# An attention and gated-MLP kernel: one 128-partition load of k over q for each pair of heads, the high part of k cast once and copied twice

## The chip, the core and the metric

The kernel runs on one core of a Trainium2 chip. The time of a kernel is the device time of one execution in microseconds (us), and lower is better. The profile shows one more execution, with its own time. It names the engines PE (TensorE matmul; PEld is its weight load), DVE (VectorE), ACT (ScalarE), POOL (GpSimd) and SP (SyncE, which here issues nearly all DMAs; its queue is shown as SPq).

## The reference

Attention with a causal mask and a bias from cumulative sums, over 8 batches of 8 heads (sequence 576, head size 64), and then a gated MLP on its output (model width 512, inner width 1024):

```python
def _attn_ref(q, k, v, s):
    scores = np.matmul(q, k.transpose(0, 1, 3, 2)) / np.sqrt(D)
    cum = np.cumsum(np.maximum(s, 0.0), axis=-1)
    bias = -(cum[:, :, :, None] - cum[:, :, None, :])
    scores = np.where(causal, -1e9, scores + np.minimum(bias, 0.0))
    scores = scores - np.max(scores, axis=-1, keepdims=True)
    attn = np.exp(scores)
    attn = attn / (np.sum(attn, axis=-1, keepdims=True) + 1e-09)
    return np.matmul(attn, v)

def _moe_ref(x, w_in, w_spatial, b_spatial, w_out):
    h = np.maximum(x @ w_in, 0.0)
    u, v = h[..., :512], h[..., 512:]
    v_n = (v - mean(v)) / np.sqrt(var(v) + 1e-06)
    v_s = np.einsum('ts,bsd->btd', w_spatial, v_n) + b_spatial[None, :, None]
    return (u * v_s) @ w_out
```

All inputs are float32 but the four MLP weights, which come as float64 and are turned into two f16 parts on the core.

## The kernel before

The 64 heads are worked in 32 **pairs** of heads, four pairs to a batch, each followed by that batch's share of the MLP. Numbers behind names are pairs (or batches): pb9 belongs to pair 4 (two heads, 8 and 9), KA1 is the second of three buffers.

**From k and q to scores.** The first three pairs (`native_tiles`) multiply k and q as float32. From pair 3 on, k and q are split into a high and a low f16 part, and the scores of a block are two matmuls over 128 rows, KA with QA and then KB with QB (L316). Rows 64 to 127 of KA and of KB both hold the high part of k; rows 0 to 63 of KB hold the low part of k; rows 61 to 63 of KA hold the cumulative sums (`aux_rows`, L214, three small DMAs). Rows 64 to 127 of QA and rows 0 to 63 of QB hold the high part of q, rows 64 to 127 of QB its low part. KA, KB, QA and QB have three buffers each, used in turn, so a buffer is free when the scores of three pairs before are done.

**Loads and splits.** `load_raw` (L226) brings k of a pair twice, to rows 64 to 127 and to rows 0 to 63 of `kraw`, and q to rows 64 to 127 of `qraw` (and to rows 0 to 63 too below pair 6, by N_CD = 6); each of these loads has 64 partitions and 288 KB. `kraw` and `qraw` have one buffer each (N_RB = 1). `split_raw` casts all 128 rows of `kraw` to KB on DVE (L251), subtracts on DVE for the low part (L255), fills KA's rows from `kraw` on ACT (L249, below pair 6) or from KB by a DMA (L257), casts q to QA on ACT (L259), fills QB's rows 0 to 63 on ACT (L261, below pair 6) or by a DMA from QA (L263), and makes the low part of q in four pieces on POOL (L239).

**Softmax and attention.** DVE adds the mask and takes the maximum (L320), ACT takes the exponential with its sum (L326), ACT and DVE write the weights as two f16 parts, pb (L335, L336), and a DMA transpose on SP's queue turns pb to pT (L341). PE multiplies pT with the two parts of v, V1 and V2 (L413; avt, L423, for the last 64 rows), and ACT and DVE write the result as xt (L429, L430). The float32 v is loaded in `fetch_v` (L272, L273) and split in `load_v` (L280).

**MLP of a batch.** vps (L457), its layer norm with hv, mv and rs (L477 to L484), split to vn on ACT and DVE (L490, L491), ups (L507), sps (L520 to L523), the gate g (L525 to L528), ops (L539) and the output. The float64 weights are loaded as words (`fetch_w64`, L158, tile wst) and turned to two f16 parts by four DVE operations (L167 to L174, tile wt), ACT operations and one POOL operation (L153); w_in is worked in eight parts, w_out in four, and all parts of w_out share one wst buffer.

**What sets the order.** Each step gets a position from a table of constants (L23), the list `plan` is sorted by it, and the program is written in that order. The scheduler of the tile framework then orders the instructions of each engine by a simulated timeline, so that the order on an engine follows both the list and the scheduler's own durations. For positions below G_END a dependency without a wait keeps the instructions of an engine behind the last one of the steps marked `first`. Each engine works its instructions strictly in the order so found, and SP issues its DMAs so too. A DMA on SP's queue also waits until the one that is eight places ahead of it has landed, since the DMAs take eight semaphores in turn.

Of the kernel before, what the change touches and what calls it, by code (L numbers as in the profile page):

```python
# [7 lines left out]
F16 = mybir.dt.float16  # L8
# [22 lines left out]
def attn_gated_mlp(ctx, tc, qT, kT, v, s, w_in, w_spT, b_sp, w_out, outT):  # L31
    nc = tc.nc
    P = 128
    NHB, D, H, S = qT.shape
    B, H = NHB // 2, 2 * H
# [77 lines left out]
    def native_tiles(pair):  # L113


        hs = slice(2 * (pair % 2), 2 * (pair % 2) + 2)
        tags = (("g1", "g2"), ("xt1", "xt2"), ("xt1", "xt2"), ("rawk", "rawq"))[pair]
        raw_tiles(pair // 2, hs, tags, (1, 2, 2, N_RB)[pair])
        first_ins["c"] = [raw_rows(pair // 2, hs, nm, 1) for nm in "kq"][1].ins
# [98 lines left out]
    def raw_tiles(hb, hs, tags=("rawk", "rawq"), bufs=1):  # L218

        for tag, nm in zip(tags, "kq"):  # L220
            raws[hb, hs.start, nm] = wk.tile([P, hs.stop - hs.start, S], F32, tag=tag, bufs=bufs, name=f"{nm}raw{hb}")

    def raw_rows(hb, hs, nm, top):
        rows = slice(64 * top, 64 * top + 64)
        if nm == "k" or top or 2 * hb + hs.start // 2 < N_CD:
            return nc.sync.dma_start(out=raws[hb, hs.start, nm][rows], in_=(kT if nm == "k" else qT)[hb, :, hs])  # L226

    def load_raw(hb, pr):
        hs = slice(2 * pr, 2 * pr + 2)
        raw_tiles(hb, hs, bufs=N_RB)  # L230
        for top in (1, 0):
            for nm in "kq":
                raw_rows(hb, hs, nm, top)

    def pieces(eng, out, in0, in1):
        for j in range(2):
            for hf in range(2):
                c = slice(hf * TH, hf * TH + TH)
                eng.tensor_tensor(out=out[:, j, c], in0=in0[:, j, c], in1=in1[:, j, c], op=ALU.subtract)  # L239

    def split_raw(hb, nm, pr):

        p = 2 * hb + pr
        i = p % 3
        raw = raws[hb, 2 * pr, nm]
        lo, hi = slice(0, 64), slice(64, 128)
        if nm == "k":
            if p < N_CD:
                nc.scalar.copy(KA[i][hi], raw[hi])  # L249
            if p < N_KA:  # L250
                nc.vector.tensor_copy(KB[i], raw)  # L251
            else:
                nc.scalar.copy(KB[i], raw)
            eng = nc.gpsimd if p < N_KP else nc.vector
            eng.tensor_tensor(out=KB[i][lo], in0=raw[lo], in1=KB[i][lo], op=ALU.subtract)  # L255
            if p >= N_CD:
                nc.sync.dma_start(out=KA[i][hi], in_=KB[i][hi])  # L257
        else:
            (nc.scalar.copy if p < N_QA else nc.vector.tensor_copy)(QA[i][hi], raw[hi])  # L259
            if p < N_CD:  # L260
                (nc.scalar.copy if p < N_QA else nc.vector.tensor_copy)(QB[i][lo], raw[lo])  # L261
            else:
                nc.sync.dma_start(out=QB[i][lo], in_=QA[i][hi])  # L263
            pieces(nc.gpsimd, QB[i][hi], raw[hi], QA[i][hi])
# [169 lines left out]
    def mlp(b):  # L434
# [32 lines left out]
        for t in range(NC5):  # L467
# [14 lines left out]
            nc.gpsimd.tensor_scalar(rs, mv[:, 1:2], 1.0e-6, None, op0=ALU.add)  # L482
# [7 lines left out]
            nc.scalar.activation(d1, hv, AF.Copy, bias=0.0, scale=SVN)  # L490
            nc.vector.scalar_tensor_tensor(out=d2, in0=hv, scalar=SVN, in1=d1, op0=ALU.mult, op1=ALU.subtract)  # L491
# [84 lines left out]
    for p in range(4):  # L576
# [5 lines left out]
        else:  # L582
            at(l, True, behind, "c", load_raw, 1, p % 2)
            for nm in "kq":
                at((0, 0, O_S2, O_S3)[p], True, split_raw, 1, nm, p % 2)
# [100 lines left out]
```

## Time and profile before

| | before |
|---|---|
| median of 3 runs | 735.04 us (731.93, 736.01, 735.04) |
| profiled execution | 736.15 us, its span 734.4 us |
| mean granted clock of TensorE | 0.944 |
| kraw loads, qraw loads | 61 and 35, 288.0 KB each |
| KA from KB, QB from QA by DMA | 26 and 26, 144.0 KB each |
| DMA in all | 119.10 MB, mean 162 GB/s |

The span goes from the first to the last instruction; 1.75 us of the profiled time lie outside of it. "Busy" is the time in which an engine has an instruction at work; an engine that is not busy waits for the one that the trace names behind an arrow. Loads of k, q and v are counted in KB of 1024 bytes, rates in units of 10^9 bytes each second.

### The profile page before, as it was taken

The numbers are of one execution on the slowest core, as the hardware profiler recorded it, in microseconds if no ns is written. First come the engines' busy times: TensorE is split into PE (matmuls) and PEld (weight loads), VectorE is DVE, ScalarE is ACT, GpSimd is POOL, SyncE is SP. The second block draws the span as 40 slices with busy tenths as digits, with TensorE's granted clock in tenths as the row PEclk, the third lists the DMA queues.
The fourth block names the chain that finished last, engine by engine and source line by source line (L and its number), as shares of the span: only waits on it lengthen the run. The fifth ranks groups of instructions, "written<-read, shape, count | busy, mean of one in ns | idle before, by whom it ended". The sixth has DMA issues, their size and how long they took to land. (4 is left out here: it accounts for less than half of the span.)

```text
span 734.4 us, 15985 instructions
## 1 busy us (share of the span) xinstructions
PE 633.7 (86%) x5696; PEld 408.8 (56%) x5696; DVE 606.4 (83%) x1660; ACT 525.1 (72%) x1334; POOL 186.5 (25%) x226
## 2 busy tenths in 40 slices
PE   4563737867656999999999999999999999999998
PEld 2232314634324577656765676476656765677576
DVE  8977998889998769898998999889988997872431
ACT  5975768667579568878787878788778888762322
POOL 7000464443022312233223322242224220100100
PEclk9986778988878999999999999999999999999999
DMA  8899957678989939898999699978996888450001
GB/s 200 193 203 213 216 148 160 110 169 184 212 189 188 203 70 188 185 206 137 213 185 227 133 188 168 237 160 170 189 231 163 159 170 184 84 109 34 33 12 65
DMA packets 243262, 119.10 MB, mean 162 GB/s; under 512 B 213887, under 2 KB 227373, under 8 KB 243182
## 3 DMA queue, kind: packets, MB, share of 16 engines
q1 hardware_dynamic: 243182, 118.08, 77.0%
q8 instruction: 45, 0.74, 0.4%
q14 instruction: 35, 0.29, 0.1%
HBM read 46.71 MB, written 9.44 MB: 76 GB/s over the span
## 5 line engine op out<-in xcount | busy, mean ns | idle before, releaser
L239 POOL TENSOR_TENSOR QB<-qraw,QA 64x288 f16<-64x288 f32 x116 | 127.5, 1129 | 321.3 <-ACT QA L259 273.4
L326 ACT ACTIVATE p<-psS,mx 128x512 f32<-128x512 f32 (+3 forms) x256 | 132.7, 524 | 50.7 <-DVE mx L320 27.0
L320 DVE CUSTOM_DVE_ANT_0 psS<-psS,mb 128x128 f32<-128x128 f32 (+3 forms) x320 | 154.2, 492 | 16.5 <-PE psS L316 13.8
L336 DVE SCALAR_TENSOR_TENSOR pb<-p,sm,pb 128x384 f16<-128x384 f32 (+3 forms) x256 | 136.3, 566 | 10.5 <-ACT pb L335 9.6
L335 ACT ACTIVATE pb<-p,sm 128x384 f16<-128x384 f32 (+3 forms) x256 | 122.7, 554 | 21.2 <-DVE sm L331 9.9
L539 PE MATMUL ops<-g,wo 128*128 128x288 f16 x768 | 108.1, 290 | 10.2 <-DVE g L525 4.4
L413 PE MATMUL av<-pT,V 128*64 128x128 f16 (+2 forms) x960 | 84.5, 294 | 34.1 <-DMA pT<-pb 28.6
L457 PE MATMUL vps<-win,xt 128*128 128x512 f16 (+1 forms) x576 | 102.7, 352 | 12.7 <-ACT p L326 7.7
L520 PE MATMUL sps<-ws,vn 128*128 128x288 f16 x768 | 108.4, 289 | 0.7 <-DVE vn L491 0.7
L507 PE MATMUL ups<-xt,win 128*128 128x288 f16 x768 | 102.4, 287 | 0.0
L316 PE MATMUL psS<-KA,QA 128*128 128x128 f16 (+3 forms) x348 | 85.4, 316 | 13.4 <-ACT p L326 11.8
L539 PEld LDWEIGHTS <-wo 128*128 128x128 f16 x768 | 74.5, 99 | 37.5 <-issue 12.0
L316 PE MATMUL psS<-KB,QB 128*128 128x128 f16 (+4 forms) x348 | 89.8, 312 | 0.4 <-DVE KB L255 0.4
L413 PEld LDWEIGHTS <-V 128*64 128x64 f16 x960 | 52.0, 116 | 66.4 <-issue 48.0
L520 PEld LDWEIGHTS <-vn 128*128 128x128 f16 x768 | 74.3, 99 | 26.3 <-issue 2.9
L507 PEld LDWEIGHTS <-win 128*128 128x128 f16 x768 | 73.4, 98 | 23.3 <-issue 2.4
L457 PEld LDWEIGHTS <-xt 128*128 128x128 f16 (+1 forms) x576 | 46.9, 103 | 60.6 <-issue 20.7
L482 POOL TENSOR_SCALAR rs<-mv 128x1 f32<-128x1 f32 x40 | 12.4, 310 | 168.1 <-DVE mv L481 154.3
L316 PEld LDWEIGHTS <-QA 128*128 128x128 f16 (+1 forms) x348 | 29.4, 102 | 39.6 <-issue 32.1
L326 ACT ACTIVATION_READ_ACCUMULATOR p<-psS,mx 128x1 f32 x256 | 51.3, 201 | 0.0
L527 ACT CAST g<-g 128x288 f16<-128x288 f32 x64 | 27.3, 427 | 31.6 <-DVE g L525 31.5
L255 DVE TENSOR_TENSOR KB<-kraw,KB 64x1152 f16<-64x1152 f32 x29 | 45.7, 1576 | 0.2
(117 smaller groups left out, 876.8 us busy)
## 6 DMA issues: line engine op xcount, KB each, us to landing
kraw<-in_kT_dram SPq DMA_DIRECT2D x61, 288.0 KB
qraw<-in_qT_dram SPq DMA_DIRECT2D x35, 288.0 KB
out_dram<-ob SPq DMA_DIRECT2D x32, 288.0 KB
vraw<-in_v_dram SPq DMA_DIRECT2D x16, 512.0 KB
wst<-in_w_in_dram SPq DMA_DIRECT2D x8, 512.0 KB
QB<-QA SPq DMA_DIRECT2D x26, 144.0 KB
KA<-KB SPq DMA_DIRECT2D x26, 144.0 KB
vraw<-in_v_dram SPq DMA_DIRECT2D x16, 128.0 KB
```

The costliest lines, as they stand in the source:

```text
L239: eng.tensor_tensor(out=out[:, j, c], in0=in0[:, j, c], in1=in1[:, j, c], op=ALU.subtract)
L255: eng.tensor_tensor(out=KB[i][lo], in0=raw[lo], in1=KB[i][lo], op=ALU.subtract)
L316: nc.tensor.matmul(ps[m, c0:c0 + w], U[i][:, g, q0:q0 + n], T[i][:, g, k0:k0 + w], start=st, stop=not st)
L320: nc.vector.tensor_tensor_reduce(out=ps[:, c0:c0 + w], in0=ps[:, c0:c0 + w], in1=mask, op0=ALU.add, op1=ALU.min, scale=-0.125, scalar=3.0e ...
L326: nc.scalar.activation(p32, ps[:, c0:c0 + w], AF.Exp, bias=mx[:, col:col + 1], scale=-1.0, accum_out=sm[:, acc:acc + 1])
L335: nc.scalar.activation(dst[:, off:off + w], p32, AF.Copy, bias=0.0, scale=sm[:, col:col + 1])
L336: nc.vector.scalar_tensor_tensor(out=dst[:, n + off:n + off + w], in0=p32, scalar=sm[:, col:col + 1], in1=dst[:, off:off + w], op0=ALU.mul ...
L413: nc.tensor.matmul(dst, V[i][:, jc, h + j], rhs, start=jc == n == 0 and q0 > 0, stop=jc == 3 and n == 2)
L457: nc.tensor.matmul(ps[m, 0:w], xx[:, c, t * P:t * P + (m.stop - m.start)], ww[:, c, NF + g * w:NF + g * w + w], start=c == n == 0, stop=c ...
L507: nc.tensor.matmul(ps[:, 0:TH], ww[:, c, fs], xx[:, c, ts], start=n == 0, stop=n == 3 * KC - 1)
L520: nc.tensor.matmul(ps[:, 0:TH], vv[:, c, fs], ww[:, c, ts], start=n == 0, stop=False)
L539: nc.tensor.matmul(ps[:, 0:TH], ww[:, f, ms], gg[:, f, ts], start=n == 0, stop=n == 3 * FC - 1)
```

## The change

For each pair from pair 3 on, the host lays k over q in one array (`kqT`), and one load of 128 partitions (576 KB, tile `raw`, two buffers) brings k to rows 0 to 63 and q to rows 64 to 127. DVE casts k once, to the tile `kh` (64 rows, one buffer); two DMAs copy kh to rows 64 to 127 of KA and of KB; DVE subtracts kh from raw for the low part. For q, ACT writes QA as before, a DMA fills QB's rows 0 to 63 for every pair, and the four POOL pieces stay. ACT's casts of L249 and L261 are gone. In the layer norm the factor 64 moves to the POOL operation that makes rs, so ACT makes the first part of vn with a copy and DVE the second with a plain subtraction. The table of constants is the same; N_CD, N_KA, N_QA, N_KP and N_RB are not used any more. Nothing else of what is computed changes.

```diff
--- before.py
+++ after.py
@@ -215,53 +215,40 @@
 
     raws = {}
 
-    def raw_tiles(hb, hs, tags=("rawk", "rawq"), bufs=1):
-
-        for tag, nm in zip(tags, "kq"):
-            raws[hb, hs.start, nm] = wk.tile([P, hs.stop - hs.start, S], F32, tag=tag, bufs=bufs, name=f"{nm}raw{hb}")
-
-    def raw_rows(hb, hs, nm, top):
-        rows = slice(64 * top, 64 * top + 64)
-        if nm == "k" or top or 2 * hb + hs.start // 2 < N_CD:
-            return nc.sync.dma_start(out=raws[hb, hs.start, nm][rows], in_=(kT if nm == "k" else qT)[hb, :, hs])
-
-    def load_raw(hb, pr):
-        hs = slice(2 * pr, 2 * pr + 2)
-        raw_tiles(hb, hs, bufs=N_RB)
-        for top in (1, 0):
-            for nm in "kq":
-                raw_rows(hb, hs, nm, top)
-
-    def pieces(eng, out, in0, in1):
-        for j in range(2):
-            for hf in range(2):
-                c = slice(hf * TH, hf * TH + TH)
-                eng.tensor_tensor(out=out[:, j, c], in0=in0[:, j, c], in1=in1[:, j, c], op=ALU.subtract)
-
-    def split_raw(hb, nm, pr):
-
-        p = 2 * hb + pr
+    def raw_tiles(hb, hs, tags):
+
+        for (tag, bufs), nm in zip(tags, "kq"):
+            raws[hb, hs.start, nm] = wk.tile([P, 2, S], F32, tag=tag, bufs=bufs, name=f"{nm}raw{hb}")
+
+    def raw_rows(hb, hs, nm):
+        src = kqT[hb, 0:64, hs] if nm == "k" else kqT[hb, 64:128, hs]
+        return nc.sync.dma_start(out=raws[hb, hs.start, nm][64:128], in_=src)
+
+    def load_raw(p):
+
+        hb, pr = divmod(p, 2)
+        raws[p] = wk.tile([P, 2, S], F32, tag="raw", bufs=2, name=f"raw{p}")
+        nc.sync.dma_start(out=raws[p], in_=kqT[hb, :, 2 * pr:2 * pr + 2])
+
+    def split_raw(nm, p):
+
+
         i = p % 3
-        raw = raws[hb, 2 * pr, nm]
+        raw = raws[p] if nm == "k" else raws.pop(p)
         lo, hi = slice(0, 64), slice(64, 128)
         if nm == "k":
-            if p < N_CD:
-                nc.scalar.copy(KA[i][hi], raw[hi])
-            if p < N_KA:
-                nc.vector.tensor_copy(KB[i], raw)
-            else:
-                nc.scalar.copy(KB[i], raw)
-            eng = nc.gpsimd if p < N_KP else nc.vector
-            eng.tensor_tensor(out=KB[i][lo], in0=raw[lo], in1=KB[i][lo], op=ALU.subtract)
-            if p >= N_CD:
-                nc.sync.dma_start(out=KA[i][hi], in_=KB[i][hi])
+            kh = wk.tile([64, 2, S], F16, tag="kh", bufs=1, name=f"kh{p}")
+            nc.vector.tensor_copy(kh, raw[lo])
+            nc.sync.dma_start(out=KA[i][hi], in_=kh)
+            nc.sync.dma_start(out=KB[i][hi], in_=kh)
+            nc.vector.tensor_tensor(out=KB[i][lo], in0=raw[lo], in1=kh, op=ALU.subtract)
         else:
-            (nc.scalar.copy if p < N_QA else nc.vector.tensor_copy)(QA[i][hi], raw[hi])
-            if p < N_CD:
-                (nc.scalar.copy if p < N_QA else nc.vector.tensor_copy)(QB[i][lo], raw[lo])
-            else:
-                nc.sync.dma_start(out=QB[i][lo], in_=QA[i][hi])
-            pieces(nc.gpsimd, QB[i][hi], raw[hi], QA[i][hi])
+            nc.scalar.copy(QA[i][hi], raw[hi])
+            nc.sync.dma_start(out=QB[i][lo], in_=QA[i][hi])
+            for j in range(2):
+                for c in (slice(0, TH), slice(TH, S)):
+                    nc.gpsimd.tensor_tensor(out=QB[i][hi, j, c], in0=raw[hi, j, c], in1=QA[i][hi, j, c],
+                                            op=ALU.subtract)
 
     vraws = {}
@@ -479,7 +466,8 @@
                 nc.sync.dma_start(out=st[0:64, 1], in_=st[64:128, 0])
                 nc.sync.dma_start(out=st[64:128, 1], in_=st[0:64, 0])
             nc.vector.bn_aggr(out=mv, in_=st if tail else st[:, 0])
-            nc.gpsimd.tensor_scalar(rs, mv[:, 1:2], 1.0e-6, None, op0=ALU.add)
+
+            nc.gpsimd.tensor_scalar(rs, mv[:, 1:2], 1.0e-6, 1.0 / (SVN * SVN), op0=ALU.add, op1=ALU.mult)
             nc.gpsimd.tensor_tensor(out=rs, in0=rs, in1=mhalf, op=ALU.pow)
             nc.vector.tensor_scalar(hv, hv, mv[:, 0:1], rs, op0=ALU.subtract, op1=ALU.mult)
             if tail:
@@ -487,8 +475,8 @@
                 d2 = wk.tile([P, w], F16, tag="tl", bufs=1, name=f"tl{b}")
             else:
                 d1, d2 = vn1[:, t], vn2[:, t]
-            nc.scalar.activation(d1, hv, AF.Copy, bias=0.0, scale=SVN)
-            nc.vector.scalar_tensor_tensor(out=d2, in0=hv, scalar=SVN, in1=d1, op0=ALU.mult, op1=ALU.subtract)
+            nc.scalar.copy(d1, hv)
+            nc.vector.tensor_tensor(out=d2, in0=hv, in1=d1, op=ALU.subtract)
             if tail:
                 for g in range(2):
                     m, gs = slice(64 * g, 64 * g + 64), slice(g * w, g * w + w)
@@ -580,9 +568,9 @@
             at(l, True, native_sel, p)
             at((-19.9, -18.9, O_S2, O_S3)[p], True, native_cum, p)
         else:
-            at(l, True, behind, "c", load_raw, 1, p % 2)
+            at(l, True, behind, "c", load_raw, p)
             for nm in "kq":
-                at((0, 0, O_S2, O_S3)[p], True, split_raw, 1, nm, p % 2)
+                at((0, 0, O_S2, O_S3)[p], True, split_raw, nm, p)
     at(-19.95, True, prefix_sums)
     at(O_I1, True, init_static, 0)
     at(O_I0, True, init_static, 1)
@@ -596,10 +584,10 @@
     for hb in range(2, NHB):
         lag = LAGS if hb < 4 else LAG
         for pr in range(2):
-            at(4 * hb + 2 * pr - O_LR + (LAGR if hb < 4 else LAG), False, load_raw, hb, pr)
+            at(4 * hb + 2 * pr - O_LR + (LAGR if hb < 4 else LAG), False, load_raw, 2 * hb + pr)
             at(4 * hb + 2 * pr - O_LD + lag, False, aux_rows, 2 * hb + pr)
             for n, nm in enumerate("kq"):
-                at(4 * hb + 2 * pr - O_LD + lag + D_LD * n, False, split_raw, hb, nm, pr)
+                at(4 * hb + 2 * pr - O_LD + lag + D_LD * n, False, split_raw, nm, 2 * hb + pr)
         at(4 * hb - O_LV + (LAGV if hb < 4 else LAG), False, fetch_v, hb)
         at(4 * hb - O_LV + (LAGV if hb < 4 else LAG), False, load_v, hb)
     for c in range(KC):
@@ -660,8 +648,7 @@
 
     B, H, S, D = inputs['q'].shape
     lay = {
-        'qT': inputs['q'].reshape(2 * B, H // 2, S, D).transpose(0, 3, 1, 2),
-        'kT': inputs['k'].reshape(2 * B, H // 2, S, D).transpose(0, 3, 1, 2),
+        'kqT': _np.concatenate([inputs[n].reshape(2 * B, H // 2, S, D).transpose(0, 3, 1, 2) for n in 'kq'], axis=1),
         'v': inputs['v'].transpose(0, 2, 1, 3).reshape(B, S, H * D),
         's': inputs['s'].reshape(B * H, S),
         'w_in': inputs['moe_w_in'],
```

As the scheduler orders the changed program anew, rows move on several engines. Three places follow.

SP's queue at the start, before. The rows stand between the loads of pairs 0 to 3 and the second attention transpose; vraw0 and vraw1 are v of the first two half-batches, wst parts of w_in, kraw2 and qraw2 belong to pair 4, pT0 is the first transpose.

```order
L158 DMA wst_328<-in_w_in_dram 128x1024
L272 DMA vraw0_330<-in_v_dram 128x4x256
L273 DMA vraw0_330<-in_v_dram 128x256
L158 DMA wst_333<-in_w_in_dram 128x1024
L341 DMA_TRANSPOSE pT0_176<-pb0_146 128x20x128
L272 DMA vraw1_514<-in_v_dram 128x4x256
L273 DMA vraw1_514<-in_v_dram 128x256
L341 DMA_TRANSPOSE pT('t', 0)_192<-pb4_0_182 128x10x128
L158 DMA wst_521<-in_w_in_dram 128x1024
L226 DMA kraw2_523<-in_kT_dram 64x1152
L226 DMA qraw2_524<-in_qT_dram 64x1152
L341 DMA_TRANSPOSE pT1_221<-pb1_194 128x20x128
```

The same place now, from the second wst load on (raw4 and raw5 are the loads of pairs 4 and 5):

```order
L158 DMA wst_331<-in_w_in_dram 128x1024
L259 DMA vraw1_512<-in_v_dram 128x4x256
L260 DMA vraw1_512<-in_v_dram 128x256
L158 DMA wst_519<-in_w_in_dram 128x1024
L231 DMA raw4_521<-in_kqT_dram 128x1152
L158 DMA wst_545<-in_w_in_dram 128x1024
L231 DMA raw5_599<-in_kqT_dram 128x1152
L158 DMA wst_601<-in_w_in_dram 128x1024
L214 DMA KA1_77<-cc_112 1x2x576 x3
L214 DMA KA2_78<-cc_112 1x2x576
L328 DMA_TRANSPOSE pT0_176<-pb0_146 128x20x128
L328 DMA_TRANSPOSE pT('t', 0)_192<-pb4_0_182 128x10x128
```

The first transpose stood behind two wst loads and v of the first half-batch; now v of the second half-batch, three more wst loads and the loads of pairs 4 and 5 stand ahead of it too, and the next transpose follows it at once.

SP's queue around the copies of pairs 6 and 7 now, where there were loads of k and q and copies from KB before (psS4 names the scores of pair 4, which read KA1):

```order
L242 DMA KA0_76<-kh6_1205 64x1152
L192 DMA wsp_st_822<-in_w_spT_dram 128x576
L243 DMA KB0_103<-kh6_1205 64x1152
L231 DMA raw8_1159<-in_kqT_dram 128x1152
L214 DMA KA1_77<-cc_112 1x2x576 x3
L247 DMA QB1_101<-QA1_74 64x1152
L242 DMA KA1_77<-kh7_1530 64x1152
L243 DMA KB1_104<-kh7_1530 64x1152
```

DVE's rows at the same time, from the cast of pair 7 to that of pair 8:

```order
L241 CAST kh7_1530<-raw7_811 64x1152
L307 ISA psS4_959,mx4_907<-psS4_959,mb4_90 128x128
L307 ISA mx4_907 128x1
L150 SCALAR_TENSOR_TENSOR ws2_121<-wsp_st_822,ws1_120 128x576
L468 BN_AGGR mv0_0_1052<-st0_0_1051 128x2
L468 BN_AGGR mv0_1_1085<-st0_1_1084 128x2
L307 ISA psS4_1001,mx4_907<-psS4_1001,mb_85 128x384
L307 ISA mx4_907 128x1
L244 TENSOR_TENSOR KB1_104<-raw7_811,kh7_1530 64x1152
L365 TENSOR_TENSOR mx4_907<-mx4_907 128x1
L317 TENSOR_SCALAR sm4_908<-sm4_908 128x4 x2
L241 CAST kh8_1708<-raw8_1159 64x1152
```

The cast to kh8 needs the one kh buffer, so it waits until both copies of kh7 have landed, and those stand behind the small KA1 loads on SP, which wait for the scores of pair 4. The wait is new: before, the cast wrote KB itself.

DVE around the last split of w_out, before (wt_1515; pb17 is the second head of pair 8):

```order
L170 SCALAR_TENSOR_TENSOR wt_1515<-wst_1513,wt_1515 128x512
L336 SCALAR_TENSOR_TENSOR pb17_2070<-p32_17_2071,sm8_1876,pb17_2070 128x384
L336 SCALAR_TENSOR_TENSOR pb17_2070<-p32_17_2071,sm8_1876,pb17_2070 128x512
L336 SCALAR_TENSOR_TENSOR pb17_2070<-p32_17_2071,sm8_1876,pb17_2070 128x128
L378 TENSOR_TENSOR mx9_2152<-mx9_2152 128x1
L336 SCALAR_TENSOR_TENSOR pb17_2070<-p32_17_2071,sm8_1876,pb17_2070 128x256
L320 ISA psS9_2344,mx9_2152<-psS9_2344,mb_85 128x384
L320 ISA mx9_2152 128x1
L330 TENSOR_SCALAR sm9_2153<-sm9_2153 128x4
L174 SCALAR_TENSOR_TENSOR wt_1515<-wst_1513,wt_1515 128x512
```

And now (wt_1499; pb16 is the first head of pair 8):

```order
L170 SCALAR_TENSOR_TENSOR wt_1499<-wst_1497,wt_1499 128x512
L318 RECIPROCAL sm8_1861<-sm8_1861 128x1
L323 SCALAR_TENSOR_TENSOR pb16_1862<-p32_16_1863,sm8_1861,pb16_1862 128x512
L307 ISA psS9_2140,mx9_2136<-psS9_2140,mb_85 128x384
L307 ISA mx9_2136 128x1
L323 SCALAR_TENSOR_TENSOR pb16_1862<-p32_16_1863,sm8_1861,pb16_1862 128x128
L323 SCALAR_TENSOR_TENSOR pb16_1862<-p32_16_1863,sm8_1861,pb16_1862 128x256
L317 TENSOR_SCALAR sm8_1861<-sm8_1861 128x4
L174 SCALAR_TENSOR_TENSOR wt_1499<-wst_1497,wt_1499 128x512
```

The last step of the split stood behind the four weights of pb17, and stands now behind those of pb16, ahead of pb17: it was DVE's row 493 and is row 471. On PE, the matmuls ops of batch 0 that read the last parts of w_out (tile ops0_11) had 24 psS, 30 av and 30 avt matmuls more ahead of them before than now: the scores and the attention of one pair. From the third ups tile of batch 1 on (ups1_10), PE has issued the same scores in both programs, and its order is nearly the same from there to the end.

More of the change, by code (lines that the diff above doesn't have):

```diff
@@ L30, in attn_gated_mlp @@
 @with_exitstack
-def attn_gated_mlp(ctx, tc, qT, kT, v, s, w_in, w_spT, b_sp, w_out, outT):
+def attn_gated_mlp(ctx, tc, kqT, v, s, w_in, w_spT, b_sp, w_out, outT):
     nc = tc.nc
     P = 128
-    NHB, D, H, S = qT.shape
-    B, H = NHB // 2, 2 * H
+    NHB, D, H, S = kqT.shape
+    B, H, D = NHB // 2, 2 * H, D // 2
     NPAIR = H // 2
@@ L116, in native_tiles @@
         hs = slice(2 * (pair % 2), 2 * (pair % 2) + 2)
-        tags = (("g1", "g2"), ("xt1", "xt2"), ("xt1", "xt2"), ("rawk", "rawq"))[pair]
-        raw_tiles(pair // 2, hs, tags, (1, 2, 2, N_RB)[pair])
-        first_ins["c"] = [raw_rows(pair // 2, hs, nm, 1) for nm in "kq"][1].ins
+        tags = ((("g1", 1), ("g2", 1)), (("xt1", 2), ("xt2", 2)), (("xt1", 2), ("xt2", 2)))[pair]
+        raw_tiles(pair // 2, hs, tags)
+        first_ins["c"] = [raw_rows(pair // 2, hs, nm) for nm in "kq"][1].ins
     def native_sel(pair):
```

## The prediction

> **What bounds the kernel now.** I read the page's shares first, then the span in 40 slices, and then busy time by stage.
>
> ```profile
> PE 633.7 (86%) x5696; PEld 408.8 (56%) x5696; DVE 606.4 (83%) x1660; ACT 525.1 (72%) x1334; POOL 186.5 (25%) x226
> PE   4563737867656999999999999999999999999998
> DVE  8977998889998769898998999889988997872431
> DMA  8899957678989939898999699978996888450001
> ```
>
> PE leads by busy time, but not everywhere. A slice is 734.4 / 40 = 18.4 us: for the first thirteen slices (239 us) PE has digits of 3 to 8, and from there 9s to the end. DVE and the DMA engines have 7s to 9s where PE has not. Cut into stages (us, then busy us of each engine with its instructions, the granted clock, the DMA share, GB/s):
>
> ```profile
> 0.00:85.00 85.00, 45.26 (x327) 23.08 (x329) 72.77 (x194) 61.55 (x145) 18.26 (x30) 0.85 0.95 201
> 85.00:239.00 154.00, 101.39 (x831) 61.07 (x829) 140.20 (x350) 110.97 (x272) 56.50 (x51) 0.82 0.80 174
> 239.00:650.00 411.00, 406.26 (x3843) 266.02 (x3842) 364.61 (x1054) 326.05 (x856) 107.45 (x136) 1.00 0.86 173
> 650.00:734.40 84.40, 80.79 (x702) 58.67 (x700) 28.82 (x64) 26.54 (x62) 4.25 (x10) 1.00 0.17 47
> ```
>
> The columns after the length are PE, PEld, DVE, ACT, POOL. Up to 85 us the DMA engines are full (0.95); to 239 us DVE is the fullest engine (140.20 of 154, 91%); from 239 to 650 us PE has 4.7 us of idle time in 411, and in the chain that ended last PE stands alone from 604 us on. So **whatever this change gives or takes must arise in the first 239 us**, and PE then carries it to the end one for one. The order of PE after that place is nearly the same in both programs, which leaves no other source. In the later stages the fewer bytes and six ACT casts can save at most those 4.7 us, and I count nothing: PE is the cover, and DVE has 411.00 - 364.61 = 46 us of room before it would show.
>
> **What the early stage waits for.** The waits between 20 and 245 us (total, times, longest), by engine and releaser:
>
> ```profile
> PE av L413 <- DMA pT<-pb: 27.2, 12, 5.6
> ACT pb L335 <- DMA pT<-pb: 6.0, 2, 4.2
> DVE KB L251 <- DMA kraw<-in_kT_dram: 4.5, 3, 1.9
> ```
>
> Transposes and loads both come late. How fast a load is depends on its shape. The first row is the DMA view from 3 to 11 us, when loads of k and q with 64 partitions are nearly all that is issued or under way; the second is from 17 to 20 us, when the loads under way are wst and v, with 128 partitions.
>
> ```profile
> DMA packets 457, 1.71 MB, mean 214 GB/s; under 512 B 85, under 2 KB 85, under 8 KB 457
> DMA packets 744, 1.04 MB, mean 345 GB/s; under 512 B 36, under 2 KB 643, under 8 KB 744
> ```
>
> The engines are full both times, so the same bytes take 1.6 times as long with 64 partitions.
>
> **Term A, the loads of the start: -4.4 us.** Issues up to 85 us, KB each:
>
> ```profile
> qraw<-in_qT_dram SPq DMA_DIRECT2D x9, 288.0 KB
> kraw<-in_kT_dram SPq DMA_DIRECT2D x7, 288.0 KB
> ```
>
> These are k and q of the pairs 0 to 4 and q of pair 5: 16 x 294,912 B = 4.72 MB, at 214 GB/s 22.0 us of full DMA engines. Now there are six such loads (8.3 us), three raw loads of 589,824 B (1.77 MB at 345 GB/s, 5.1 us) and three copies of 147,456 B for pair 3 (at 214 GB/s, for want of a nearer row, 2.1 us): 15.5 us, or **6.6 us less**. That is the most; the least is nothing, where DVE hides it. DVE has no room in most of the start and has some in other parts:
>
> ```profile
> 10.00:15.00 5.00, 5.00 (x19) 2.22 (x18) 3.50 (x8) 3.31 (x6) 1.30 (x3) 1.00 1.03 218
> 25.00:30.00 5.00, 2.94 (x9) 1.22 (x9) 5.00 (x19) 4.53 (x15) 0.00 (x0) 1.00 0.80 139
> 55.00:60.00 5.00, 1.07 (x11) 1.07 (x12) 2.10 (x7) 1.01 (x2) 0.00 (x0) 0.58 0.95 196
> ```
>
> From 25 to 30 us DVE is full, and an earlier load buys nothing there. From 10 to 15 and from 55 to 60 us DVE is idle for 1.5 and 2.9 us while the DMA engines are full. I take these two holes, 4.4 us, as what earlier data can close.
>
> A rule of the Trainium skill (page "DMA: Bandwidth & Descriptors", section "Rules for kernel authors") says that two transfers to disjoint halves of the partitions serialize, because both use the same 16 engines, and advises one 128-partition transfer. Read strictly, only bytes count then, and the start would save (4.72 - 3.98) MB at 201 GB/s = 3.7 us in place of 6.6. The trace speaks for more, since its two rates differ.
>
> **Term B, the splits from 85 to 239 us: -1.3 us.** raw has two buffers, so a load can be issued while the pair before is still being split: DVE's three waits of 4.5 us go. The work on DVE and POOL stays the same, by these rows:
>
> ```profile
> L251 DVE CAST KB<-kraw 128x1152 f16<-128x1152 f32 x29 | 23.4, 809 | 6.0 <-DMA kraw<-in_kT_dram 6.0
> L255 DVE TENSOR_TENSOR KB<-kraw,KB 64x1152 f16<-64x1152 f32 x29 | 45.7, 1576 | 0.2
> L491 DVE SCALAR_TENSOR_TENSOR vn<-hv,vn 128x512 f16<-128x512 f32 x32 | 21.8, 682 | 2.6 <-ACT vn L490 2.5
> L528 DVE TENSOR_TENSOR g<-g,g 128x288 f16<-128x288 f32 x64 | 33.0, 516 | 7.7 <-ACT g L527 7.7
> ```
>
> The cast has half the partitions and as many elements on each, so I leave it at 809 ns. The subtraction has the same form. The plain subtraction for vn is not in the trace with 512 columns; by the ns for each column of L255 (1576 / 1152 = 1.37) it takes 700 ns, by those of L528 (516 / 288 = 1.79) 917, by those of the cast (0.70) 360, against 682 now. Four of them (batch 0) lie before 239 us: from -1.3 to +0.9 us; I take 0, by L255, the nearest in form. ACT's copy for vn and the second constant of POOL's rs change nothing that I can read off any row; ACT is 72% busy in this stage (110.97 of 154.00) and POOL 37%, which hides some tenths on each.
>
> New is the **wait for the one kh buffer**: the cast to kh(p+1) waits until both copies of kh(p) have landed, and DVE with all its masks, weights and norms queues behind it. The tightest place is kh8, eleven rows after kh7 on DVE. SP's issue times and the way of a small DMA are in these rows (SP's two, then DVE's that uses the copy):
>
> ```profile
> 61.64 2.32 SPq L214 DMA_DIRECT2D KA<-cc  x3
> 150.81 0.59 SPq L480 DMA_DIRECT2D st<-st  x1
> 152.61 0.21 DVE L481 BATCH_NORM_AGGREGATE mv<-st 128x2 f32<-128x12 f32 x1
> ```
>
> The KA1 loads can only be issued after the last scores of pair 4, about when DVE masks them. Then: three KA loads 2.3 us, QB 0.6, and KA 0.6 and KB 0.6 for kh7, then 1.8 us from the last issue to use (152.61 - 150.81, an upper end) and 147,456 B / 201 GB/s = 0.7 us more: 6.6 us. Against it DVE has the last mask row of pair 4 with its reading, the subtraction and two or three small rows: five at its mean of 606.4 / 1660 = 0.365 us, and 1.2 us more for the subtraction, 3.0 us. **The stall is 3.6 us at the dearest**, less if SP is early. Later pairs have 20 rows and more between their casts, so I price only this one, at 3.2 (SP's 0.4 us of slack taken off): -4.5 + 3.2 = -1.3. The ends are -4.5 and +3.6.
>
> **Term C, the last split of w_out: -2.5 us.** The last w_out split gates the ops of batch 0, after which PE has no more idle time to speak of:
>
> ```profile
> 229.43 0.54 PE L539 MATMUL ops<-g,wo 128*128 128x288 f16 x3 [0.16 <-POOL wo L153]
> 234.29 2.83 PE L539 MATMUL ops<-g,wo 128*128 128x288 f16 x12
> 606.50 0.54 PE psS L316 x4
> 672.36 1.10 PE av L413 x18
> 625.80 0.47 PE avt L423 x30
> ```
>
> On DVE that split stands 493 - 471 = 22 rows earlier, 22 x 0.365 = 8.0 us. But in return the matmuls of one pair are behind it instead of ahead: by the last three rows 24 x 0.135 + 30 x 0.061 + 0.47 = 5.5 us, work that PE did while it had to wait anyway. -8.0 + 5.5 = **-2.5**; the ends are -8.0 (PE finds other holes for it) and 0.
>
> **The sum.** -4.4 - 1.3 - 2.5 = -8.2 us against the profiled execution's own 736.15 (span 734.4, and 1.75 around it): **728.0 us**. That execution lies 1.1 above the median of the runs, 735.04, within their spread.
>
> **Rivals.**
>
> *Nothing comes through.* DVE, 86% busy to 85 us and 91% to 239 us, hides A, and C cancels, since both move the same work around one engine: only -1.3 is left, 734.9. For it: DVE is full in most 5-us pieces of the start, and its work is unchanged. Against it: its holes are where DMA is full.
>
> *The change doesn't cut DMA work.* The loads of a pair fall from 864 to 576 KB, but the copies inside the core grow from 288 to 432 KB from pair 6 on, and from none to 432 for pairs 3 to 5. If a copy costs as much as a 64-partition load, a pair of the first three goes from 4 x 294,912 B / 214 = 5.5 us to 1.7 + 2.1 = 3.8, and the gain of A shrinks to 5 us or less for three pairs, spread beyond 85 us. This ends between the first rival and the forecast, near 732; the forecast's range holds it.
>
> *Slower: the first transpose is held back.* SP works in order, and pT0 now stands behind 8.06 MB of loads in place of 4.80 MB. The arrivals of transposes on PE, and SP's first issues of them:
>
> ```profile
> 29.98 0.32 PE L413 MATMUL av<-pT,V 128*64 128x384 f16 x1 [1.55 <-DMA pT<-pb]
> 43.67 1.17 PE L413 MATMUL av<-pT,V 128*64 128x384 f16 x16 [1.73 <-DMA pT<-pb]
> 84.84 3.36 PE L413 MATMUL av<-pT,V 128*64 128x384 f16 x29 [1.67 <-DMA pT<-pb]
> 24.92 3.20 SPq L341 DMA_TRANSPOSE pT<-pb  x1
> 29.41 2.45 SPq L341 DMA_TRANSPOSE pT('t', 0)_192<-pb  x1
> ```
>
> The 3.26 MB more take 16.2 us at 201 GB/s, so pT0 (29.98) may land at 46.2, and behind it the tail transpose and pT1, with 2.45 and 3.20 us of issue, at 51.9 in place of 43.67: 8.2 us late. ACT's writing of pb waits for such a landing (the row of 6.0 us above), DVE waits for ACT, and the delay goes through. It decides if **pT1 lands later than 43.67**. Then A is +8.2 in place of -4.4, and B and C stay: 736.15 + 8.2 - 1.3 - 2.5 = **740.6**. Against it: the 3.26 MB are not extra, they stood between later transposes before, and by the last transpose of the start (84.84) both programs have loaded about as much, 10.4 and 10.3 MB by the shapes in SP's order. The loads ahead are also faster now.
>
> *Better than forecast.* A in full (-6.6), no stall at kh8 (B -4.5), C as it is: 722.6, and with C in full (-8.0) 717.0.
>
> **Chances.** A measurement of this kernel can tell about 0.5% from no change, 3.7 us: 731.4 to 738.7. Forecast, with the rival of unchanged DMA work beside its upper end: 0.50 (722.6 to 731.4). Better still: 0.08. Nothing comes through: 0.24. Slower by the first transpose: 0.18 (738.7 to 744). So faster 0.58, same 0.24, slower 0.18. The range goes from 718, near the sum of the best ends, to 741, which takes in the slower rival's own time; beyond both ends about 0.15 to 0.2 is left.
>
> **What would show it.** A right: loads of raw at over 300 GB/s, DVE's holes at 10 to 15 and 55 to 60 us smaller, pT1 on PE before 43.67 and pT7 before 84.84. A wrong: pT1 later than that, with a longer wait of ACT on pT. B right: no wait of the cast on a load from 85 us on, and one wait of some 3 us on a copy of kh at kh8; wrong: many such waits, 1 us and more at each cast. C right: ops0_11 on PE near 220.6 (234.29 less 8.0 and less the 5.7 of A and B), and PE gapless behind it. The whole is wrong if PE shows more than 5 us of idle time after its ops of batch 0, or if the distance from there to the end differs from that of before by more than the 5.5 us that were moved.

## The result, and the profile after

The changed kernel is **slower**: 759.54 us median (751.79 to 763.07, 4 runs) against 735.52 us (731.93 to 738.17, 4 runs) for the kernel before, a ratio of 1.0315 (95% interval 1.0224 to 1.0407). The profiled execution took 763.07 us, its span is 761.3 us, 26.9 us longer than before.

The page of the changed kernel has DVE busy for 8 us less, but PE for 21 us longer with as many matmuls (654.9 us against 633.7, 5696 each), and PE's digits differ where it was gapless before:

```profile
PE 654.9 (86%) x5696; PEld 414.2 (54%) x5696; DVE 598.3 (79%) x1660; ACT 519.8 (68%) x1328; POOL 181.9 (24%) x226
PE   4764457987689998989899898989998999999998
DVE  9879997687986979689787887789879897963331
DMA  9988756577687787957777767968995776451001
```

Busy time by stage of the changed kernel (columns as in the prediction):

```profile
0.00:85.00 85.00, 49.46 (x342) 26.93 (x342) 74.81 (x197) 58.60 (x143) 22.42 (x29) 0.79 0.89 208
85.00:239.00 154.00, 114.77 (x849) 65.32 (x843) 129.69 (x340) 106.68 (x264) 56.96 (x56) 0.80 0.72 165
239.00:650.00 411.00, 382.81 (x3545) 245.81 (x3545) 342.75 (x988) 306.67 (x802) 95.08 (x125) 0.98 0.75 159
```

Up to 239 us PE did more than before (49.5 + 114.8 us against 45.3 + 101.4). From 239 to 650 us its idle time rose from 4.7 to 28.2 us, and DVE's from 46 to 68 us, while the DMA engines have less to do (0.75 against 0.86). So the loss is neither in the start nor a matter of bytes.

The first ups matmuls of a batch are a milestone that both traces show. First of before, batch 1 and batch 7, then of the changed kernel:

```profile
257.48 3.11 PE L507 MATMUL ups<-xt,win 128*128 128x288 f16 x24
693.35 11.93 PE L507 MATMUL ups<-xt,win 128*128 128x288 f16 x96
```

```profile
246.86 1.63 PE L495 MATMUL ups<-xt,win 128*128 128x288 f16 x12
720.45 11.93 PE L495 MATMUL ups<-xt,win 128*128 128x288 f16 x96
```

At batch 1 the changed kernel is **10.6 us ahead**; from there to batch 7 it needs 473.6 us where the kernel before needs 435.9, **37.7 us more**; -10.6 + 37.7 = +27.1, the whole difference. A little of the 10.6 is moved work: 35 matmuls of scores and attention that stood ahead of this milestone before come behind it now, and at the third ups tile, from which on PE's order is nearly the same, the lead is 9.3 us (252.08 against 261.41).

The stretch between the two milestones, before and then now, splits the 37.7 us:

```profile
257.48:693.35 435.87, 431.13 (x4110) 284.73 (x4108) 369.03 (x1064) 330.24 (x865) 103.07 (x132) 1.00 0.79 161
246.86:720.45 473.59, 447.27 (x4143) 288.73 (x4142) 378.46 (x1091) 339.48 (x888) 101.06 (x138) 0.98 0.69 147
```

PE's idle time grew from 4.7 to 26.3 us, and PE was busy 16.1 us longer for nearly as many matmuls, at a granted clock of 0.98 in place of 1.00.

The group of the cast to kh says what DVE stood still for (busy, mean ns, then the idle time just before it with its releasers), and the view of waits says how much of it lies between 239 and 650 us (total, times, longest):

```profile
L241 DVE CAST kh<-raw 64x1152 f16<-64x1152 f32 x29 | 22.8, 785 | 47.9 <-DMA KB<-kh 37.5 <-DMA KA<-kh 5.9 <-issue 3.7
```

```profile
DVE kh L241 <- DMA KB<-kh: 31.0, 12, 5.1
DVE kh L241 <- DMA KA<-kh: 5.9, 2, 3.6
DVE kh L241 <- issue: 3.7, 1, 3.7
PE psS L303 <- ACT q L313: 15.8, 10, 2.5
```

15 of the 19 casts of that stage wait, 40.6 us in all. This is DVE's time and not PE's, so that it lies near the 37.7 us of loss proves nothing yet; the paced kernel below is the test. PE's longest wait there (the last line) is for ACT's exponentials, which wait for DVE's maxima. One pair in the middle, pair 23 and the cast of pair 24, on DVE, POOL and SP, and at the end what waited behind it on ACT and PE (start, us, what, idle time before):

```profile
442.51 0.75 DVE L241 CAST kh<-raw 64x1152 f16<-64x1152 f32 x1 [0.57 <-DMA KB<-kh]
454.81 3.14 SPq L328 DMA_TRANSPOSE pT<-pb  x1
456.57 1.35 DVE L244 TENSOR_TENSOR KB<-raw,kh 64x1152 f16<-64x1152 f32 x1
456.59 4.74 POOL L250 TENSOR_TENSOR QB<-raw,QA 64x288 f16<-64x288 f32 x4 [15.07 <-ACT QA L246]
458.04 1.37 SPq L328 DMA_TRANSPOSE pT('t', 20)_5643<-pb  x1
461.35 0.36 SPq L231 DMA_DIRECT2D raw<-in_kqT_dram  x1
462.40 0.53 SPq L242 DMA_DIRECT2D KA<-kh  x1
463.03 0.54 SPq L243 DMA_DIRECT2D KB<-kh  x1
467.87 0.75 DVE L241 CAST kh<-raw 64x1152 f16<-64x1152 f32 x1 [3.69 <-issue]
468.92 0.47 ACT L313 ACTIVATE p<-psS,mx 128x256 f32<-128x256 f32 x1 [3.60 <-DVE mx L307]
470.76 0.38 PE L303 MATMUL psS<-KA,QA 128*128 128x512 f16 x1 [2.30 <-ACT q L313]
```

The cast of pair 23 runs at 442.5, but KA and KB of that pair are free only when the scores of pair 20 are done, at 456 us (counting DVE's mask rows against the program's order, the last of pair 20 starts at 455.9). On SP the copies stand behind two transposes and behind the raw load of pair 25, which waits for POOL's pieces; they are issued at 462.4 and 463.0, behind 576 KB, and 4.8 us after the last issue the next cast goes, after 3.7 us of standstill. (For this one cast the trace names no releaser; that it waited for the copies is read from the one kh buffer and from the rows of its neighbours.) By the same count the first mask row of pair 24 comes at 526.0: no score needed its cast for another 58 us, and yet all of DVE's rows behind it waited. ACT waited 3.60 us for one of them and PE 2.30 us for ACT, and from 470 to 475 us the granted clock is 0.68, where it was 1.00 from 440 to 470. The chain that ended last passes through the same kind of wait at the cast of pair 29:

```profile
565.52 0.36 SPq L231
565.93 4.88 DMA KA<-kh
570.81 0.55 issue
571.36 0.75 DVE kh L241
```

### The profile page after: what moved, and what is told of

It reads as the page before. It is cut to its first block, busy times and chain, and to the rows that moved or that the text cites. A ratio compares the mean times of both kernels' runs of the same rounds, so it can differ in the third digit from the quotient of the medians.

```text
span 761.3 us, 15918 instructions
## 1 busy us (share of the span) xinstructions
PE 654.9 (86%) x5696; PEld 414.2 (54%) x5696; DVE 598.3 (79%) x1660; ACT 519.8 (68%) x1328; POOL 181.9 (24%) x226
## 2 busy tenths in 40 slices
DMA packets 243038, 114.83 MB, mean 151 GB/s; under 512 B 213471, under 2 KB 226957, under 8 KB 242958
## 5 line engine op out<-in xcount | busy, mean ns | idle before, releaser
L250 POOL TENSOR_TENSOR QB<-raw,QA 64x288 f16<-64x288 f32 x116 | 118.6, 1052 | 261.2 <-ACT QA L246 151.6
L313 ACT ACTIVATE p<-psS,mx 128x128 f32<-128x128 f32 (+3 forms) x256 | 132.7, 523 | 60.2 <-DVE mx L307 35.6
L323 DVE SCALAR_TENSOR_TENSOR pb<-p,sm,pb 128x384 f16<-128x384 f32 (+3 forms) x256 | 133.2, 555 | 7.7 <-ACT pb L322 7.3
L444 PE MATMUL vps<-win,xt 128*128 128x512 f16 (+1 forms) x576 | 107.0, 359 | 14.6 <-POOL win L153 9.7
L400 PE MATMUL av<-pT,V 128*64 128x128 f16 (+2 forms) x960 | 91.0, 300 | 32.4 <-DMA pT<-pb 20.5
L508 PE MATMUL sps<-ws,vn 128*128 128x288 f16 x768 | 113.0, 298 | 3.3 <-DVE g L513 2.6
L495 PE MATMUL ups<-xt,win 128*128 128x288 f16 x768 | 106.2, 291 | 0.0
L303 PE MATMUL psS<-KB,QB 128*128 128x128 f16 (+3 forms) x348 | 91.5, 314 | 0.0
L444 PEld LDWEIGHTS <-xt 128*128 128x128 f16 (+1 forms) x576 | 47.5, 104 | 64.3 <-issue 27.1
L470 POOL TENSOR_SCALAR rs<-mv 128x1 f32<-128x1 f32 x40 | 16.0, 401 | 199.6 <-DVE mv L468 174.5
L241 DVE CAST kh<-raw 64x1152 f16<-64x1152 f32 x29 | 22.8, 785 | 47.9 <-DMA KB<-kh 37.5
L515 ACT CAST g<-g 128x288 f16<-128x288 f32 x64 | 27.1, 428 | 40.5 <-DVE g L513 40.4
L303 PEld LDWEIGHTS <-QA 128*128 128x128 f16 (+1 forms) x348 | 30.0, 103 | 45.3 <-issue 39.1
```

Of the source, the lines that this page charges most:

```text
L250: nc.gpsimd.tensor_tensor(out=QB[i][hi, j, c], in0=raw[hi, j, c], in1=QA[i][hi, j, c], op=ALU.subtract)
L303: nc.tensor.matmul(ps[m, c0:c0 + w], U[i][:, g, q0:q0 + n], T[i][:, g, k0:k0 + w], start=st, stop=not st)
L313: nc.scalar.activation(p32, ps[:, c0:c0 + w], AF.Exp, bias=mx[:, col:col + 1], scale=-1.0, accum_out=sm[:, acc:acc + 1])
L323: nc.vector.scalar_tensor_tensor(out=dst[:, n + off:n + off + w], in0=p32, scalar=sm[:, col:col + 1], in1=dst[:, off:off + w], op0=ALU.mul ...
L400: nc.tensor.matmul(dst, V[i][:, jc, h + j], rhs, start=jc == n == 0 and q0 > 0, stop=jc == 3 and n == 2)
L444: nc.tensor.matmul(ps[m, 0:w], xx[:, c, t * P:t * P + (m.stop - m.start)], ww[:, c, NF + g * w:NF + g * w + w], start=c == n == 0, stop=c ...
```

## The experiments

Each was timed beside the kernel before; ratios are against that. The kernel before took 738.1 to 739.5 us at the median in these sessions and 735.5 beside the changed kernel, so 3 or 4 us between runs of different sessions say little. "The changed kernel" is the base unless another is named. Every edit also makes the scheduler order the rows of all engines anew, so a run shows an edit together with its new order.

**Two kh buffers** (`e1_kh2_g1`) and its control (`e2_g1`). The first theory, K, was that the number of kh buffers decides.

```diff
-            kh = wk.tile([64, 2, S], F16, tag="kh", bufs=1, name=f"kh{p}")
+            kh = wk.tile([64, 2, S], F16, tag="kh", bufs=2, name=f"kh{p}")
...
-            g32 = wk.tile([P, TH], F32, tag="g32", bufs=2, name=f"g32_{b}_{f}{hf}")
+            g32 = wk.tile([P, TH], F32, tag="g32", bufs=1, name=f"g32_{b}_{f}{hf}")
```

> The changed kernel with two kh buffers (the room comes from the gate's g32 tile, one buffer in place of two). Theory K (each cast to kh waits on DVE for the copies of the pair before, some 40 us of it where PE was the bound): the 43.4 us of idle time ahead of the cast that end with a copy fall under 5 us, PE is gapless again from about 250 us on, and the time is 759.5 - 37.7 = about 722 us (the 37.7 us are what the span from the first ups of batch 1 to that of batch 7 grew by). Rival M (the wait on DVE is only where the time shows; the new order of the transposes and copies on SP, or DMA traffic, costs it in any case): DVE's wait moves to another line and the time stays above 745 us.

> The changed kernel with one g32 buffer and still one kh buffer: the control for the other edit. If the gate's second buffer matters, this run is slower than the changed kernel by the same amount that the run with two kh buffers loses; expected 759 to 764 us, the waits for a copy of kh as in the changed kernel (about 43 us).

Measured: 766.63 us with two kh buffers (ratio 1.0364, 1.0328 to 1.0400), 761.76 us with the g32 edit alone (1.0291, 1.0247 to 1.0335), where the casts wait 41.2 us in all. Theory K in this form fell: the second buffer wins nothing. The wait is still at the cast:

```profile
L241 DVE CAST kh<-raw 64x1152 f16<-64x1152 f32 x29 | 24.8, 855 | 50.9 <-DMA KB<-kh 19.6 <-DMA raw<-in_kqT_dram 19.0 <-issue 12.2
```

The program's order shows why. With one buffer the subtraction of a pair (from pair 10 on) stands 16 to 44 rows behind its cast; with two buffers 53 to 85 rows. The scheduler used the freedom to pull the casts one pair further ahead, up to the next things that hold them, the raw load and the copies of two pairs before, and DVE waits there (19.0 and 19.6 us). Rival M was right in its number (above 745 us); but the wait stayed at the cast's line, with other releasers, and its cause was not M's, as the paced run below shows.

**Raw loads in halves, with two kh buffers** (`e5_kh2_half`).

```diff
-        nc.sync.dma_start(out=raws[p], in_=kqT[hb, :, 2 * pr:2 * pr + 2])
+        for r in (slice(0, 64), slice(64, 128)):
+            nc.sync.dma_start(out=raws[p][r], in_=kqT[hb, r, 2 * pr:2 * pr + 2])
```

> Two kh buffers and one g32 buffer as before, and each load of raw issued as two loads of 64 partitions (k, then q). Theory A (the start gained because 128-partition loads run at about 345 GB/s and 64-partition loads at 214): the first ups of batch 1 comes 3 to 7 us later than in the run with one load, the DMA share rises, and the time is 726 to 730 us. Rival (the shape of the load is worth nothing, the start gained by the order and by the second raw buffer): within 1.5 us of the run with one load.

Measured: 765.27 us (1.0343, 1.0303 to 1.0382), no different from its base of 766.63; the 726 to 730 us expected had taken theory K for granted. The time can't tell theory A from its rival here, where DVE's waits set it later. The first ups of batch 1 came at 249.86 us against 244.31 in its base, 5.5 us later, inside theory A's 3 to 7; but this is one trace of each order, and with the paced cast (`e9_pace_half`, below) the same edit moved that milestone the other way. So it settles nothing.

**The cast in place** (`e6_inplace`).

```diff
-            kh = wk.tile([64, 2, S], F16, tag="kh", bufs=1, name=f"kh{p}")
+            kh = KB[i][lo]
```

> The changed kernel without a kh tile: the cast goes to rows 0 to 63 of KB itself (three buffers), the copies start there, and the subtraction overwrites them when the copies have landed. Theory K: the cast waits for nothing new, but the subtraction on DVE now waits for the copies of its own pair, 2 to 5 us each, if it stands close behind the cast, so DVE loses 25 pairs x 2 to 5 us again in the worst case: 745 to 770 us; if the scheduler sets the subtraction far behind the cast, about 722 us. Rival M: above 745 us in any case, with no wait of DVE on a copy of kh.

Measured: 743.53 us (1.0071, 1.0035 to 1.0106), 16 us less than the changed kernel and outside both expected ranges. The cast now needs KB, so it stands behind the scores that free KB, and waits for nothing; the subtraction waits instead, 23.7 us in all, half of the former wait:

```profile
L241 DVE CAST KB<-raw 64x1152 f16<-64x1152 f32 x29 | 24.5, 844 | 0.0
L244 DVE TENSOR_TENSOR KB<-raw,KB 64x1152 f16<-64x1152 f32 x29 | 39.6, 1365 | 23.7 <-DMA KB<-KB 23.6
```

Rival M's number was missed too, if narrowly: with less waiting on DVE came less time. This led to theory P, on the place of the cast.

**The cast paced** (`e7_pace`). One dependency without a wait keeps the cast on DVE behind the last mask row of the pair three before.

```diff
+                masked[pair] = nc.vector.tensor_tensor_reduce(...).ins
...
-            nc.vector.tensor_copy(kh, raw[lo])
+            ins = nc.vector.tensor_copy(kh, raw[lo]).ins
+            if p - 3 in masked:
+                tc.add_manual_dep(ins, masked[p - 3].name, nosync, reason="pace")
```

> The changed kernel (one kh buffer) with one dependency without a wait: on DVE the cast to kh of a pair stands behind the last mask row of the pair three before, which is where the cast to KB stood of itself, since KB had to be free. Two kh buffers did not help, so theory K in its first form is out. Theory P (place: the cast is now free of KB, so the scheduler pulls it ahead, to right behind the copies of the pair before by its own durations; on the chip these land some 5 us later, and DVE stands still in front of a row that nobody needs for 30 us): the waits of the cast fall from 47.9 us to under 8 us, PE has under 10 us of idle time from 239 to 650 us, and the time is 722 to 730 us. Rival R (ring: kh, raw, KA and POOL's pieces form a chain that is too long for a pair, wherever the cast stands): DVE's waits stay above 20 us and the time above 745 us.

Measured: **722.88 us** (0.9789, 0.9730 to 0.9848), with one kh buffer, the same copies and the same loads: 36.7 us less than the changed kernel, and faster than the kernel before. The cast waits no more, and PE is gapless again:

```profile
L242 DVE CAST kh<-raw 64x1152 f16<-64x1152 f32 x29 | 22.9, 789 | 0.0
```

```profile
239.00:650.00 411.00, 406.93 (x3926) 268.15 (x3925) 372.49 (x1080) 330.88 (x874) 105.50 (x132) 1.00 0.80 166
```

The same pairs in its trace as above (23 and 24). The copies still stand behind a raw load on SP, but they were issued sooner after the cast, and the next cast comes 11 us after the last issue instead of 4.8:

```profile
431.78 0.75 DVE L242 CAST kh<-raw 64x1152 f16<-64x1152 f32 x1
437.69 0.62 SPq L232 DMA_DIRECT2D raw<-in_kqT_dram  x1
438.41 0.53 SPq L246 DMA_DIRECT2D KB<-kh  x1
449.48 0.75 DVE L242 CAST kh<-raw 64x1152 f16<-64x1152 f32 x1
```

Theory P held and rival R fell. In the order, the cast of the next pair stands 37 to 61 rows behind a subtraction from pair 8 on, where the changed kernel has 8 to 35 and the kernel before 37 to 57: the dependency puts the cast back about where it was before the change. PE's share of the loss went with it: between the same two milestones (241.69 and 679.73) PE is idle for 3.8 us and busy for 434.2, at a granted clock of 1.00.

**The copies first on SP** (`e8_copyfirst`; O_LR is 7.25 in place of 7.334 too, so that the load is written behind the copies).

```diff
-        nc.sync.dma_start(out=raws[p], in_=kqT[hb, :, 2 * pr:2 * pr + 2])
+        ins = nc.sync.dma_start(out=raws[p], in_=kqT[hb, :, 2 * pr:2 * pr + 2]).ins
+        if p - 2 in copied:
+            tc.add_manual_dep(ins, copied[p - 2].name, nosync, reason="pace")
...
-            nc.sync.dma_start(out=KB[i][hi], in_=kh)
+            copied[p] = nc.sync.dma_start(out=KB[i][hi], in_=kh).ins
```

> The changed kernel with both copies of kh of a pair ahead of the raw load of two pairs later on SP (a dependency without a wait, and the load's position 0.084 later): the copies no longer stand behind a load that waits for POOL's pieces, nor behind its 576 KB in the DMA queues. Rival H (it is SP's order that makes the copies late): DVE's waits for copies of kh fall from 43.4 us to under 15 us, and the time to 730 to 742 us. Theory P: the copies land some 3 us earlier, but the cast still stands close behind them in an order made with shorter durations, so a part of the waits stays, 15 to 35 us, and the time is 742 to 757 us.

Measured: 735.37 us (0.9981, 0.9951 to 1.0012), in the range of rival H; the cast's waits fell to 23.0 us, in the range of theory P.

```profile
L244 DVE CAST kh<-raw 64x1152 f16<-64x1152 f32 x29 | 23.1, 796 | 23.0 <-DMA KB<-kh 14.0 <-DMA KA<-kh 9.0
```

So each theory has one of its two signs, and the run speaks for a part of both: with the copies first on SP, and in the order that this edit gave, 24 us are won; the cast still stands close behind the copies, and 12.5 us are left to the paced kernel.

**Both edits together** (`e11_pace_copyfirst`).

> The paced kernel with the copies of kh ahead of the raw load on SP too. With the cast paced its wait was 0.0 us, so theory P says that nothing is left to gain: 720 to 726 us, the same as the paced kernel within 0.5%. Rival H (late copies also hold back the scores): 3 us or more faster than the paced kernel.

Measured: 722.71 us (0.9753, 0.9689 to 0.9817), the same as the paced kernel, and rival H fell: with the cast in its place, the late copies cost nothing.

**Two kh buffers, paced** (`e12_pace_kh2`, the edits of `e1_kh2_g1` and `e7_pace`).

> Two kh buffers and one g32 buffer, with the paced cast. Theory P (the place of the cast decides, not the number of buffers): the same waits as the paced kernel with one buffer (near 0) and the same time, 720 to 726 us, 40 us or more below the run with two kh buffers and no pace. Rival (with two buffers something else, g32 or the sharing of the gate, costs the time): above 735 us.

Measured: 728.16 us (0.9866, 0.9838 to 0.9894), the cast's idle time 0.0. It is 38.5 us below the same buffers without the pace, near the 40 expected. The 5 us above the paced kernel lie outside what was expected; the g32 edit that made the room may cost them (alone it cost 2.2 us, within the spread there), which was not tried apart.

**The paced kernel with half loads** (`e9_pace_half`, the edit of `e5_kh2_half`) and **with one raw buffer** (`e10_pace_raw1`, bufs=1 for the tag raw) take two terms of the prediction apart.

> The paced kernel with each raw load as two loads of 64 partitions. Theory A (the shape of the loads is worth some 4 us at the start): 3 to 7 us slower than the paced kernel with one load, and the first ups of batch 1 later by as much. Rival: the same within 2 us.

> The paced kernel with one raw buffer in place of two. Term B of the prediction (the second buffer takes the casts' waits for a load away, 4.5 us from 85 us on): the cast waits 4 to 10 us for raw loads in all, mostly ahead of 250 us, and the time is 726 to 733 us. Rival (the second buffer is worth nothing once the cast is paced): 721 to 725 us.

Measured: half loads 732.62 us (0.9914, 0.9877 to 0.9950), 9.7 us above the paced kernel, more than expected. But the loss is not where theory A puts it. The first ups of batch 1 came at 236.37 us against 241.69, 5.3 us earlier and not 3 to 7 later; from there to the first ups of batch 2 the half loads take 91.26 us against 76.26, and behind that both run alike (403.9 and 402.6 us to the end). In that one stretch PE is idle for 9.4 us in place of 0.9, in part ahead of transposes (6.1 us), at a granted clock of 0.93. So the 9.7 us are those of the shape together with what it moved, and they say nothing of the start.

One raw buffer: 720.37 us (0.9732, 0.9677 to 0.9786), not slower than with two, and its casts wait for nothing (0.0 us, where 4 to 10 were expected), so the second buffer is worth nothing once the cast is paced.

**The layer norm's part alone, on the kernel before** (`e4_vn`).

> The kernel before with the layer norm's part of the change alone (the factor 64 in POOL's operation for rs, a copy on ACT, a plain subtraction on DVE). All theories: no difference beyond 0.5%, 733 to 739 us; DVE's subtraction for vn at 682 ns before should be 600 to 750 ns.

Measured: 739.22 us against 738.89 (1.0015, 0.9978 to 1.0052): nothing. The subtraction took 681 ns against 682 before.

## Why the prediction was wrong

- **The bound** (before 239 us whatever arises, then PE carries it on): right for the kernel before, wrong as a limit for the changed one. "Whatever this change gives or takes must arise in the first 239 us" took PE's cover as given. DVE has 46 us of idle time in that stage, and the new wait used 40.6 us in front of rows that PE depends on; PE waited in turn: the sign that I had named, more than 5 us of idle time on PE behind the ops of batch 0, came with 26.3 us between the milestones. A cover of idle time in sum says nothing about a wait that comes in order, a pair at a time.
- **Term A** (-4.4): the rates were right, the size is not shown. In the changed kernel the stretch from 25.5 to 29.0 us, with raw, wst and v loads under way, ran at 337 GB/s; DVE's hole at 10 to 15 us went from 3.50 to 4.96 us busy, that at 55 to 60 from 2.10 to 5.00. But other holes opened: from 10 to 35 us DVE is busy for 21.9 us against 23.4 before, and up to 85 us for 74.8 against 72.8, 2.0 us more and not 4.4. The two runs with half loads moved the milestone of batch 1 in opposite ways (5.5 us later, 5.3 us earlier). The Trainium skill's rule that half transfers serialize ("DMA: Bandwidth & Descriptors", "Rules for kernel authors") advises one 128-partition load; the rates here agree with the advice. The 3.7 us by bytes alone were my own reading of it, and it does not hold: with the same bytes, half loads kept the DMA engines busy for longer (last section).
- **Term B** (-1.3): the waits for a load did go (none from 85 us on), but not by the second raw buffer, since `e10_pace_raw1` has none either. At kh8, which I priced at 3.2 us, the wait was 0.56 us; pair 9 had 5.88 us.
- **Term C** (-2.5): right in its sign and about in its size. The matmul of ops that stood at 234.29 us before runs at 218.88 now, 15.4 us earlier, against the 13.7 foreseen (220.6); with 5.5 us of matmuls moved behind it 9.9 us are left, and the milestone shows 10.6. The terms foresaw 8.2 for the start. Which of A, C and the new order gave it, no run takes apart.
- **The step that failed**: "Later pairs have 20 rows and more between their casts, so I price only this one". This put the wait of all pairs behind the eighth at nothing; measured, it is 46.5 of the 47.9 us on DVE. The distance was read from cast to cast (28 to 69 rows from pair 10 on, 10 to 29 us in the trace), but the copies don't start with the cast: they start when the scores of the pair three before set KA free, wait on SP behind a load, and let the next cast go about 5 us after their issue. From the subtraction, which is released at the same moment, the next cast is only 8 to 35 rows away. And I took the place of the cast as harmless, though the order showed it ahead of its use by more than a pair. Where the cast wrote KB itself, KB held it back; kh took that hold away.
- **Rivals**: none of them was it. The first transpose was late (issued at 29.33 in place of 24.92), but the next one was on PE at 42.63, ahead of the 43.67 that I had named as the point; so this rival fell; the time went past its 740.6 us by another road. The rival on unchanged DMA work fell too: 114.83 MB against 119.10, and the DMA queue's packets took 68.0% of 761.3 us against 77.0% of 734.4, 48 us less of all 16 engines.
- **Vn's plain subtraction**: 683 ns against 700 taken.

## What to carry to other kernels

A tile that frees an operation from its buffer also frees the scheduler to move it ahead, and on an engine that works in order an early row that waits holds up all the others: ask of each new wait what releases its source, not how far apart two of its kind stand. Where a wait sits in front of work that is not needed yet, try its place (one dependency without a wait) before more buffers: here two buffers gave nothing and the place gave 36.7 us. Idle time of an engine in sum is no cover for a wait that returns with every pair.

## What the runs showed of the hardware

Loads of 64 partitions moved their bytes more slowly than loads of 128. From 25 to 30 us, behind the same loads of raw, wst and v, the paced kernel moved 306 GB/s with whole loads (DMA share 0.93) and 238 with half loads (0.90). Over the whole program the same bytes took 72.8% of 720.6 us with whole loads and 74.6% of 731.5 with half loads, 21 us more of all 16 engines.

A copy of 144 KB inside the core that was issued just behind a load of 576 KB took 4.88 us to land (the chain's row at 565.93). From the last issue of such copies to the next cast it was 4.8 us (463.03 to 467.87), where I had put 2.5.

The granted clock of PE was 0.68 from 470 to 475 us, just behind a gap of 2.30 us in its work, and 0.98 between the milestones, where the paced kernel, with 3.8 us of gaps there, had 1.00. What of the 16.1 us of longer busy time is due to the clock was not tried apart.
